# MoE 1's first eight units on whole float32 weights and values, their high and low parts made later

## The chip, the cores and the metric

One Trainium2 chip, one NeuronCore of it (core 0). The metric is the device time of one execution in microseconds (us), the median of the runs. Engines are named as the profile names them: PE multiplies matrices (PEld is its loading of weights, which overlaps), DVE, ACT and POOL work on vectors, SP issues most of the DMA transfers.

## The reference, cut to what matters

```python
# attention: 4 batches, 8 heads, 576 positions, 64 columns a head; heads 0-3 see a window of 32,
# heads 4-7 every fourth position of the last 128
scores = where(mask, q @ k.T / 8, -1e9);  attn = softmax(scores) ;  x = (attn @ v)  -> 2304 x 512
# MoE 1 (w_in 512 x 2048, w_out 2048 x 512, weights arrive as float64)
h = x @ w_in;   g = maximum(h, 0) + alpha * minimum(h, 0);   x = g @ w_out
# MoE 2 (other weights, float64 too)
h = x @ w_in;   g = (a0 + a1 h + a2 h^2 + a3 h^3) / (1 + |b0||h| + |b1|h^2 + 1e-6);   out = g @ w_out
```

## The kernel before

**Three parts, overlapped.** Tokens are cut into 8 chunks of 288 for attention and MoE 1 (`u` = 0 to 7) and 6 chunks of 384 for MoE 2. Attention of one chunk is 4 jobs, one for each pair of heads (`attention_job`). The 2048 columns of `w_in` (rows of `w_out`) are 16 blocks of 128 (`f`). A unit of MoE 1 is one (u, f): 12 matmuls that make `h` (L520), a leaky ReLU on ACT and DVE (L640, L643), and, `LAG1 = 2` units later, 12 matmuls that add into `y` (L673). `SEQ` (L621) is the order of the 128 units: f 0 to 7 for chunk 0 (units n = 0 to 7), f 0 to 7 for chunk 1 (n = 8 to 15), f 8 to 15 for chunk 0 (n = 16 to 23), f 8 to 15 for chunk 1 (n = 24 to 31), then chunks 2 to 7 whole.

**Split products.** Every float32 operand is split into a high part (a copy rounded to float32r, `wh`, `x1h`, `g..h`) and a low part (the rest, `wl`, `x1l`, `g..l`), and a product is three float32r matmuls: low weight by high value, high by low, high by high (L516 to L524 and L669 to L676). So one unit has 4 x 3 matmuls for h and 4 x 3 for y, each 128 x 128 by 288 columns.

**Weights.** They arrive as float64, and a "turn" decodes one: `w64_load` (d) brings the words of w_in for block f and of w_out for block f - 2 into a buffer `raw` (there are `RAWB = 2`, 1 MB each), `w64_exponent` (x, ACT L145) scales the upper words, `w64_sign`, `w64_upper`, `w64_lower` (j, J, i, DVE L151, L158, L164) put the float32 bits into `w`, `w64_hi` (h, ACT L187) and `w64_lo` (l, DVE L197) make `wh` and `wl`. Turns 0 to 17 are MoE 1's, 18 to 35 MoE 2's, whose result goes back to DRAM. h of block f wants turn f, y of block f wants turn f + 2. A `tick` is one step of each kind (L213), and `PACE` (L87) says how many ticks a unit gets: 0.75 up to n = 13, 0.55 up to n = 21, then 0.23. Turns 0 to 3 are decoded in `head()`, in the order of the string `HEAD`.

**Order.** Attention's steps are put into half units by tables (`STEPS`, `EARLY`). Chunk 1's four jobs must end before n = 8. From these program lines a scheduler makes the order on each engine; each engine's queue runs in that order. Rows named `h_0_3` are h of u = 0, f = 3.

Of the kernel before, what the change touches and what calls it, by code (L numbers as in the profile page):

```python
# [22 lines left out]
def tile_attention_moe_moe2(  # L23
# [14 lines left out]
    nc = tc.nc  # L38
# [40 lines left out]
    SPLIT = True  # L79
    NORM_DVE = 3  # L80
    PRE = 3
    W32B = 2
    KEEP = 1
    MAN = ''
    MAN_FROM = 0
    MAN_TO = 128
    PACE = ((14, 0.75), (22, 0.55), (128, 0.23))  # L87

    cst = ctx.enter_context(tc.tile_pool(name="cst", bufs=1))
    wpool = ctx.enter_context(tc.tile_pool(name="wpool", bufs=NF))  # L90
# [68 lines left out]

    def w64_lower(n):
        t, w = raws[n]
        nc.vector.scalar_tensor_tensor(  # L164
            w, t[:, :, 0], 29, w, op0=ALU.logical_shift_right, op1=ALU.bitwise_or
        )
        raws[n] = w.bitcast(F32)
        moe, parts = turns[n]
        if moe == 2:
            for i, (f, part) in enumerate(parts):  # L170
                nc.sync.dma_start(
                    w2f[f, :, part * DM : (part + 1) * DM],
                    w[:, i * DM : (i + 1) * DM].bitcast(F32),
                )

    def w_tiles(moe, f):
        wh[moe, f] = wpool.tile([P, 2 * DM], F32R, tag="wh", name=f"wh{moe}_{f}")
# [2 lines left out]
    def w64_hi(n):  # L180
        moe, parts = turns[n]
        if moe == 1:
            for i, (f, part) in enumerate(parts):
                if (1, f) not in wh:
                    w_tiles(1, f)
                s = slice(part * DM, (part + 1) * DM)
                nc.scalar.activation(  # L187
                    wh[1, f][:, s], raws[n][:, i * DM : (i + 1) * DM], AF.Copy
                )

    def w64_lo(n):
# [86 lines left out]
    def attention_job(mem, u, hp, bk, eng=nc.sync, split=False):  # L278
# [224 lines left out]
        yield  # L503
        if u not in x1:
            x1[u] = x1_tiles(u)
        xh, xl, pxv = x1[u][0][:, hp, :], x1[u][1][:, hp, :], px[:, :C1]
        if dil:
            xh = xh.rearrange("p (i r) -> p r i", r=4)
            xl = xl.rearrange("p (i r) -> p r i", r=4)
            pxv = pxv.rearrange("p (r i) -> p r i", r=4)  # L510
        nc.scalar.activation(xh, pxv, AF.Copy)
        nc.vector.tensor_tensor(xl, pxv, xh.bitcast(F32), op=ALU.subtract)  # L512
        yield


# [10 lines left out]
    if True:  # L526
# [102 lines left out]
        def moe1_h(n):  # L629
            u, f = SEQ[n]  # L630
            ph = bank("h", 2, f"h1_{u}_{f}")
            h_matmuls(ph, C1, wh[1, f], wl[1, f], *x1[u])
            h = ph[:, :C1]
            r = mo1.tile([P, C1], F32, tag="r1", name=f"r1_{u}_{f}")
            ghi, glo = pair(f"g1_{u}_{f}", C1)
            g_tiles[n] = (ghi, glo)
            sg, sa = side[:, f : f + 1], salpha[:, f : f + 1]

# [340 lines left out]
```

## Time and profile before

| what | value |
|---|---|
| device time, median of 3 runs | 977.42 us (972.84 to 978.70) |
| profiled execution, device time | 978.13 us |
| profiled execution, span from first to last instruction | 976.4 us |
| mean granted clock of PE over the span | 0.979 of 2.4 GHz |
| busy share of the span: PE, DVE, ACT, POOL | 96%, 68%, 65%, 22% |

All times in the views count from the start of the span. An instruction's busy time on PE, DVE and ACT includes the end of its pipeline, which overlaps the next instruction of the same engine; the distance between two starts is therefore shorter than the duration printed. A row of a timeline joins like instructions that follow each other ("x4"). PEclk 1.00 is 2.4 GHz, 0.50 is 1.2 GHz.

### The profile page before, as it was taken

The numbers are of one execution on the slowest core, as the hardware profiler recorded it, in microseconds if no ns is written. First come the engines' busy times: TensorE is split into PE (matmuls) and PEld (weight loads), VectorE is DVE, ScalarE is ACT, GpSimd is POOL, SyncE is SP. The second block draws the span as 40 slices with busy tenths as digits, with TensorE's granted clock in tenths as the row PEclk, the third lists the DMA queues.
The fourth block names the chain that finished last, engine by engine and source line by source line (L and its number), as shares of the span: only waits on it lengthen the run. The fifth ranks groups of instructions, "written<-read, shape, count | busy, mean of one in ns | idle before, by whom it ended". The sixth has DMA issues, their size and how long they took to land.

```text
span 976.4 us, 18434 instructions
## 1 busy us (share of the span) xinstructions
PE 937.6 (96%) x6704; PEld 874.4 (90%) x6704; DVE 666.2 (68%) x1578; ACT 632.1 (65%) x1575; POOL 212.7 (22%) x257
## 2 busy tenths in 40 slices
PE   6789899999999999999999999999999999999998
PEld 5678799889899999999999999999999999999996
DVE  2888885556456555554435679877777788777776
ACT  3876665656455565564545578777677776777765
POOL 2000000001000010000112345434343343343332
PEclk7799999999999999999999999999999999999999
DMA  7656535563634535322134432002030020020000
GB/s 182 162 177 178 201 117 161 137 196 97 188 115 119 184 112 162 124 83 83 50 109 136 153 112 66 1 33 65 1 94 4 31 67 1 33 65 1 34 1 33
DMA packets 93899, 94.41 MB, mean 97 GB/s; under 512 B 40176, under 2 KB 81648, under 8 KB 93808
## 3 DMA queue, kind: packets, MB, share of 16 engines
q1 hardware_dynamic: 87360, 83.78, 28.1%
q0 software_dynamic: 6448, 9.45, 3.8%
q8 instruction: 53, 0.87, 0.4%
q14 instruction: 38, 0.31, 0.1%
HBM read 69.48 MB, written 23.72 MB: 95 GB/s over the span
## 4 chain that ended last, share of the span: by engine, by line
PE 83%; ACT 5%; DMA 5%; DVE 4%; issue 1%; SPq 1%; POOL 0%; POOLq 0%; ACTq 0%; DVEq 0%
PE h L520 39%; PE o L892 20%; PE y L673 17%; DMA raw<-in_moe_w_out_dram 3%; PE px L499 2%; PE pp L448 2%; ACT pr L427 1%; PE ps L405 1%; DMA hd<-in_q_dram 1%; PE ps L393 1%; ACT hd L427 1%; DVE w L158 1%; DVE wl L197 1%; DVE w L164 1%; PE pk L356 1%
## 5 line engine op out<-in xcount | busy, mean ns | idle before, releaser
L520 PE MATMUL h<-x1h,wl 128*128 128x288 f32 x512 | 159.3, 312 | 7.0 <-DVE g_0l L649 2.4
L520 PE MATMUL h<-x1l,wh 128*128 128x288 f32 x512 | 154.2, 301 | 0.0
L520 PE MATMUL h<-x1h,wh 128*128 128x288 f32 x512 | 153.5, 300 | 0.0
L643 DVE SCALAR_TENSOR_TENSOR h<-h,salpha,r 128x288 f32<-128x288 f32 x128 | 66.9, 523 | 112.7 <-ACT r L640 112.6
L520 PE MATMUL h<-x2h,wl 128*128 128x384 f32 x384 | 130.4, 340 | 0.0
L520 PE MATMUL h<-x2h,wh 128*128 128x384 f32 x384 | 130.0, 339 | 0.0
L520 PE MATMUL h<-x2l,wh 128*128 128x384 f32 x384 | 129.6, 338 | 0.0
L640 ACT ACTIVATE r<-h,side 128x288 f32<-128x288 f32 x128 | 63.9, 499 | 98.3 <-PE h L520 98.0
L437 POOL TENSOR_TENSOR pr<-pr,sm 128x480 f32<-128x480 f32 (+2 forms) x20 | 23.9, 1197 | 467.5 <-DVE sm L435 416.8
L520 PEld LDWEIGHTS h<-x1h,wl 128*128 128x128 f32 x512 | 98.2, 192 | 11.2 <-DVE g_0l L649 2.6
L824 POOL TENSOR_SCALAR qq<-hh,babs 128x384 f32<-128x384 f32 x96 | 56.7, 591 | 225.3 <-ACT hh L822 225.2
L827 POOL TENSOR_TENSOR qq<-qq,w 128x384 f32<-128x384 f32 x96 | 97.5, 1016 | 8.3 <-POOL qq L824 0.5
L520 PEld LDWEIGHTS h<-x1h,wh 128*128 128x128 f32 x512 | 98.8, 193 | 0.1
L520 PEld LDWEIGHTS h<-x1l,wh 128*128 128x128 f32 x512 | 98.5, 192 | 0.3 <-DVE x1l L512 0.2
L822 ACT ACTIVATE hh<-h 128x384 f32<-128x384 f32 x96 | 47.2, 492 | 62.7 <-PE h L520 62.7
L829 DVE TENSOR_TENSOR t<-h,t 128x384 f32<-128x384 f32 x96 | 53.5, 557 | 48.1 <-ACT t L828 47.6
L520 PEld LDWEIGHTS h<-x2h,wl 128*128 128x128 f32 x384 | 72.0, 188 | 4.0
L520 PEld LDWEIGHTS h<-x2l,wh 128*128 128x128 f32 x384 | 72.1, 188 | 3.6
L838 ACT ACTIVATE w<-qq 128x384 f32<-128x384 f32 (+1 forms) x98 | 50.8, 519 | 33.5 <-POOL qq L827 33.5
L520 PEld LDWEIGHTS h<-x2h,wh 128*128 128x128 f32 x384 | 72.0, 187 | 0.0
L846 DVE TENSOR_TENSOR qq<-qq,w 128x384 f32<-128x384 f32 (+1 forms) x98 | 54.2, 553 | 24.4 <-ACT w L841 24.1
L427 ACT ACTIVATE pr<-pr,mx 128x96 f32<-128x96 f32 (+2 forms) x182 | 65.1, 360 | 5.9 <-DVE mx L419 5.7
(356 smaller groups left out, 2550.2 us busy)
## 6 DMA issues: line engine op xcount, KB each, us to landing
raw<-in_moe_w_in_dram SPq DMA_DIRECT2D x32, 512.0 KB
raw<-in_moe_w_out_dram SPq DMA_DIRECT2D x32, 512.0 KB
w2f<-w SPq DMA_DIRECT2D x32, 256.0 KB
w<-w2f SPq DMA_DIRECT2D x16, 512.0 KB
x2h<-x2hi POOLq DMA_DIRECT2D x6, 768.0 KB, 5.0
x2l<-x2lo POOLq DMA_DIRECT2D x6, 768.0 KB, 6.3
out_dram<-o SPq DMA_DIRECT2D x15, 256.0 KB
tq<-in_q_dram SPq DMA_DIRECT2D x28, 72.0 KB
```

The lines of the kernel that those rows point to most:

```text
L427: nc.scalar.activation(pr[:, j, :], pr[:, j, :], AF.Exp, scale=-1.0, bias=mx[:, j : j + 1], accum_out=sm[:, j : j + 1],)
L520: nc.tensor.matmul(ph[:, :n], lhsT=w_[:, c * P : (c + 1) * P], rhs=x_[:, c, :], start=(i == 0), stop=(i == 3 * KD - 1),)
L640: nc.scalar.activation(r, h, AF.Identity, scale=sg)
L643: nc.vector.scalar_tensor_tensor(h, h, sa, r, op0=ALU.mult, op1=ALU.max)
L673: nc.tensor.matmul(ys[c][:, :C1], lhsT=w_[:, s], rhs=g_, start=begin and i == 0, stop=end and i == 2,)
L822: nc.scalar.activation(hh, h, AF.Square)
L824: nc.gpsimd.tensor_scalar(qq, hh, babs, 1.0 + 1e-6, op0=ALU.mult, op1=ALU.add)
L827: nc.gpsimd.tensor_tensor(qq, qq, w, op=ALU.add)
L829: nc.vector.tensor_tensor(t, h, t, op=ALU.mult)
L838: nc.scalar.activation(w[:, s], qq[:, s], AF.Abs_reciprocal_sqrt, scale=2.0**-44)
L846: nc.vector.tensor_tensor(qq[:, s], qq[:, s], w[:, s], op=ALU.mult)
L892: nc.tensor.matmul(o2[c][i], lhsT=g_, rhs=w_, start=(f == 0 and j == 0), stop=(f == NF - 1 and j == 2),)
```

## The change

Blocks f = 0 to 7 (`FPN = FH = 8`) are first kept as whole float32: `w64_lower` writes its last bits not in place but into a tile `w1_f` (`whole`), in two halves of 512 columns, and `w64_hi` and `w64_lo` leave these blocks out. Chunk 0's attention result is one float32 tile `x1f` without a low part. The units n = 0 to 7 multiply whole float32 operands: one matmul where there were three, for h and for y, and `g` has no low part. From n = 4 on, `w_split` makes `wh` and `wl` of each block, and `x1_split` makes the two parts of chunk 0, which its second half (n = 16 to 23) uses. The buffer `w` is single (`W32B` 2 to 1). `PACE` changes: 0.75 up to n = 7, 0.25 up to n = 15, 0.75 up to n = 23, then 0.22.

```diff
-    W32B = 2
+    W32B = 1
...
-    PACE = ((14, 0.75), (22, 0.55), (128, 0.23))
+    PACE = ((8, 0.75), (16, 0.25), (24, 0.75), (128, 0.22))
+    FPN = FH
...
     def w64_lower(n):
         t, w = raws[n]
-        nc.vector.scalar_tensor_tensor(
-            w, t[:, :, 0], 29, w, op0=ALU.logical_shift_right, op1=ALU.bitwise_or
+        moe, parts = turns[n]
+        lower = lambda to, c: nc.vector.scalar_tensor_tensor(
+            to, t[:, c, 0], 29, w[:, c], op0=ALU.logical_shift_right, op1=ALU.bitwise_or
         )
         raws[n] = w.bitcast(F32)
-        moe, parts = turns[n]
+        if any(moe == 1 and f < FPN for f, _ in parts):
+            for i, (f, part) in enumerate(parts):
+                c = slice(i * DM, (i + 1) * DM)
+                if f < FPN:
+                    if (f, 0) not in whole:
+                        whole_tile(f)
+                    lower(whole[f, part].bitcast(I32), c)
+                else:
+                    lower(w[:, c], c)
+        else:
+            lower(w, slice(None))
...
+    def whole_tile(f):
+        t = wpool.tile([P, 2 * DM], F32, tag="wh", name=f"w1_{f}")
+        whole[f, 0], whole[f, 1] = t[:, :DM], t[:, DM:]
+
+    def w_split(f, part):
+        w = whole.pop((f, part))
+        s = slice(part * DM, (part + 1) * DM)
+        nc.scalar.activation(wh[1, f][:, s], w, AF.Copy)
+        nc.vector.tensor_tensor(
+            wl[1, f][:, s], w, wh[1, f][:, s].bitcast(F32), op=ALU.subtract
+        )
...
             for i, (f, part) in enumerate(parts):
+                if f < FPN:
+                    continue
...
-        nc.vector.tensor_tensor(xl, pxv, xh.bitcast(F32), op=ALU.subtract)
+        if u:
+            nc.vector.tensor_tensor(xl, pxv, xh.bitcast(F32), op=ALU.subtract)
...
-            h_matmuls(ph, C1, wh[1, f], wl[1, f], *x1[u])
             h = ph[:, :C1]
+            if n < FPN:
+                for i, c in enumerate(HPS):
+                    nc.tensor.matmul(
+                        h, lhsT=whole[f, 0][:, c * P : (c + 1) * P],
+                        rhs=x1[u][0][:, c, :],
+                        start=(i == 0), stop=(i == KD - 1),
+                    )
+            else:
+                h_matmuls(ph, C1, wh[1, f], wl[1, f], *x1[u])
...
-            at_half(n + 1, 1, lo)
+            if n >= FPN:
+                at_half(n + 1, 1, lo)
...
             for c in range(KD):
+                if n < FPN:
+                    nc.tensor.matmul(
+                        ys[c][:, :C1], lhsT=whole[f, 1][:, c * P : (c + 1) * P],
+                        rhs=ghi, start=begin, stop=end,
+                    )
+                    continue
...
+        def x1_split(c):
+
+            x, a, b = x1[0][0], *x1s
+            nc.scalar.activation(a[:, c, :], x[:, c, :], AF.Copy)
+            nc.vector.tensor_tensor(
+                b[:, c, :], x[:, c, :], a[:, c, :].bitcast(F32), op=ALU.subtract
+            )
+            if c == KD - 1:
+                x1[0] = (a, b)
...
+        for f in range(FPN):
+            at_half(f + 4, 0, lambda f=f: w_split(f, 0))
+            at_half(f + 5, 1, lambda f=f: w_split(f, 1))
+        for c in range(KD):
+            at_half(FPN + 2 + c, 1, lambda c=c: x1_split(c))
```

How the engines' orders move is shown at three places; line numbers of after are its own.

On PE, where chunk 0's last attention products (px) end and MoE 1's first unit (h_0_0) begins; before:

```order
L499 MATMUL px_2_466<-hd_2_2_106,hd_2_1_105 64x72 x6
L520 MATMUL h_0_0_606<-x1h_430,wl_0_247 128x288
L520 MATMUL h_0_0_606<-x1l_431,wh_0_246 128x288
L520 MATMUL h_0_0_606<-x1h_430,wh_0_246 128x288
L520 MATMUL h_0_0_606<-x1h_430,wl_0_247 128x288
L520 MATMUL h_0_0_606<-x1l_431,wh_0_246 128x288
```

And at the same place after (w_0 is the whole block 0, x1f the whole attention result):

```order
L529 MATMUL px_3_444<-hd_3_2_102,hd_3_1_101 64x72 x6
L668 MATMUL h_0_0_609<-x1f,w_0_195 128x288 x2
L529 MATMUL px_2_453<-hd_2_2_106,hd_2_1_105 64x72 x6
L382 MATMUL pq_0_493<-ident,tq_0_420 128x96 x3
L668 MATMUL h_0_0_609<-x1f,w_0_195 128x288
L386 MATMUL pk_0_494<-ident,tk_0_421 128x80 x4
L668 MATMUL h_0_0_609<-x1f,w_0_195 128x288
L668 MATMUL h_0_1_674<-x1f,w_1_309 128x288
L435 MATMUL ps_0_512<-kT_0_502,qT_0_503 64x96 x10
L668 MATMUL h_0_1_674<-x1f,w_1_309 128x288 x3
L668 MATMUL h_0_2_719<-x1f,w_2_382 128x288 x4
```

Twelve matmuls of h_0_0 became four, and they stand partly ahead of the last px.

On DVE, from the decoding of turn 3 to the first masks of chunk 1's attention (ISA rows); before:

```order
L197 TENSOR_TENSOR wl_2_447<-w_2_361,wh_2_446 128x512
L197 TENSOR_TENSOR wl_0_247<-w_2_361,wh_0_246 128x512
L151 TENSOR_SCALAR w_3_455<-raw_415 128x1024
L512 TENSOR_TENSOR x1l_431<-px_3_457,x1h_430 128x4x72
L512 TENSOR_TENSOR x1l_431<-px_2_466,x1h_430 128x4x72
L158 SCALAR_TENSOR_TENSOR w_3_455<-raw_415,w_3_455 128x1024
L164 SCALAR_TENSOR_TENSOR w_3_455<-raw_415,w_3_455 128x1024
L643 SCALAR_TENSOR_TENSOR h_0_0_606<-h_0_0_606,salpha,r_0_0_619 128x288
L151 TENSOR_SCALAR w_4_654<-raw_481 128x1024
L197 TENSOR_TENSOR wl_3_485<-w_3_455,wh_3_484 128x512
L197 TENSOR_TENSOR wl_1_357<-w_3_455,wh_1_356 128x512
L419 ISA pr_0_506,mx_0_507<-ps_0_509,masks_122 128x96
```

and after:

```order
L154 TENSOR_SCALAR w_3_442<-raw_411 128x1024
L161 SCALAR_TENSOR_TENSOR w_3_442<-raw_411,w_3_442 128x1024
L168 SCALAR_TENSOR_TENSOR w_3_465<-raw_411,w_3_442 128x512
L168 SCALAR_TENSOR_TENSOR w_1_309<-raw_411,w_3_442 128x512
L154 TENSOR_SCALAR w_4_648<-raw_468 128x1024
L449 ISA pr_0_509,mx_0_510<-ps_0_512,masks_122 128x96
```

The subtractions for wl and x1l are gone from here, the last step of the turn is two halves, and the first h is no longer waited for ahead of the masks.

On DVE where h of unit 16 (h_0_8) is worked on; before:

```order
L643 SCALAR_TENSOR_TENSOR h_1_7_1417<-h_1_7_1417,salpha,r_1_7_1430 128x288
L158 SCALAR_TENSOR_TENSOR w_15_1466<-raw_1392,w_15_1466 128x1024
L649 SCALAR_TENSOR_TENSOR g_1_7l<-h_1_7_1417,side,g_1_7h 128x288
L164 SCALAR_TENSOR_TENSOR w_15_1466<-raw_1392,w_15_1466 128x1024
L643 SCALAR_TENSOR_TENSOR h_0_8_1449<-h_0_8_1449,salpha,r_0_8_1462 128x288
L151 TENSOR_SCALAR w_16_1555<-raw_1470 128x512
L197 TENSOR_TENSOR wl_15_1473<-w_15_1466,wh_15_1472 128x512
L197 TENSOR_TENSOR wl_13_1333<-w_15_1466,wh_13_1332 128x512
L649 SCALAR_TENSOR_TENSOR g_0_8l<-h_0_8_1449,side,g_0_8h 128x288
```

and after:

```order
L168 SCALAR_TENSOR_TENSOR w_12_1316<-raw_1259,w_12_1316 128x1024
L694 SCALAR_TENSOR_TENSOR g_1_7l<-h_1_7_1238,side,g_1_7h 128x288
L227 TENSOR_TENSOR wl_12_1324<-w_12_1316,wh_12_1323 128x512
L688 SCALAR_TENSOR_TENSOR h_0_8_1284<-h_0_8_1284,salpha,r_0_8_1297 128x288
L227 TENSOR_TENSOR wl_10_1111<-w_12_1316,wh_10_1110 128x512
L694 SCALAR_TENSOR_TENSOR g_0_8l<-h_0_8_1284,side,g_0_8h 128x288
L154 TENSOR_SCALAR w_13_1391<-raw_1320 128x1024
L161 SCALAR_TENSOR_TENSOR w_13_1391<-raw_1320,w_13_1391 128x1024
L688 SCALAR_TENSOR_TENSOR h_0_9_1330<-h_0_9_1330,salpha,r_0_9_1343 128x288
```

Where turn 15 stood, turn 12 stands now, three turns later; and the first step of a turn (L154) stands behind both subtractions of the turn before, where it stood ahead of them.

## Rows read from the trace of the kernel before

**Rows 1.** Page, parts 1 and 4: busy shares; shares of the last chain.

```profile
PE 937.6 (96%) x6704; PEld 874.4 (90%) x6704; DVE 666.2 (68%) x1578; ACT 632.1 (65%) x1575; POOL 212.7 (22%) x257
...
PE 83%; ACT 5%; DMA 5%; DVE 4%; issue 1%; SPq 1%; POOL 0%; POOLq 0%; ACTq 0%; DVEq 0%
```

**Rows 2.** Windows: start:end, length, busy us (count) per engine, clock, DMA.

```profile
core 0: us, PE busy (x) PEld busy (x) DVE busy (x) ACT busy (x) POOL busy (x), PEclk, DMA share, GB/s
0.00:37.08 37.08, 24.58 (x223) 21.15 (x223) 19.09 (x95) 21.98 (x80) 4.91 (x17) 0.69 0.74 174
37.08:91.62 54.54, 44.71 (x399) 40.10 (x397) 47.01 (x120) 39.92 (x113) 0.00 (x0) 0.90 0.55 167
91.62:124.02 32.40, 27.30 (x195) 25.79 (x195) 29.07 (x49) 19.79 (x41) 0.00 (x0) 1.00 0.62 208
124.02:150.93 26.91, 26.91 (x219) 26.68 (x220) 19.16 (x40) 15.65 (x38) 0.00 (x0) 1.00 0.39 119
150.93:188.52 37.59, 36.13 (x343) 34.15 (x341) 23.28 (x84) 24.36 (x81) 0.00 (x0) 0.95 0.48 134
...
400.00:500.00 100.00, 99.90 (x940) 96.07 (x940) 48.61 (x181) 55.30 (x182) 8.41 (x7) 1.00 0.24 72
```

**Rows 3.** Waits of PE from 37 to 130 us: total, times, longest.

```profile
PE h L520 <- DVE g_0l L649: 2.4, 1, 2.4
PE y L673 <- ACT g_3h L646: 2.3, 1, 2.3
```

**Rows 4.** Last chain from 92 to 125 us: start, us, what.

```profile
103.03 0.38 SPq L131
...
103.47 5.95 DMA raw<-in_moe_w_out_dram
...
109.50 1.15 ACT raw L145
...
115.32 0.38 SPq L131
```

**Rows 5.** Last chain from 31 to 49 us, at chunk 0's last attention steps.

```profile
34.06 1.04 ACT wh L187 x2
...
35.44 1.71 PE px L499 x24
```

**Rows 6.** Timeline of DVE in unit 14: start, duration, instruction, tile, shape.

```profile
115.78 0.69 DVE L151 TENSOR_SCALAR w<-raw 128x1024 int32<-128x1024 int32 x1
116.38 1.29 DVE L197 TENSOR_TENSOR wl<-w,wh 128x512 fp32r<-128x512 f32 x2
117.59 1.22 DVE L158 SCALAR_TENSOR_TENSOR w<-raw,w 128x1024 int32<-128x1024 int32 x1
118.72 0.51 DVE L649 SCALAR_TENSOR_TENSOR g_5l<-h,side,g_5h 128x288 fp32r<-128x288 f32 x1
119.15 1.22 DVE L164 SCALAR_TENSOR_TENSOR w<-raw,w 128x1024 int32<-128x1024 int32 x1
120.28 0.52 DVE L643 SCALAR_TENSOR_TENSOR h<-h,salpha,r 128x288 f32<-128x288 f32 x1
```

**Rows 7.** Timeline of PE: float32r matmuls at half clock, then at full clock.

```profile
38.20 0.44 PE L520 MATMUL h<-x1l,wh 128*128 128x288 f32 x1
38.45 0.44 PE L520 MATMUL h<-x1h,wh 128*128 128x288 f32 x1
...
130.22 0.29 PE L520 MATMUL h<-x1h,wh 128*128 128x288 f32 x1
130.35 0.29 PE L520 MATMUL h<-x1h,wl 128*128 128x288 f32 x1
```

**Rows 8.** Timeline and chain of PE: float32 products (warm, ps) and transposes (pp).

```profile
1.60 5.48 PE L573 MATMUL warm<-ident 128*128 128x128 f32 x24 [1.60 <-POOL ident masks.py:199]
42.85 1.04 PE L405 MATMUL ps<-kT,qT 64*64 64x96 f32 x20
...
142.84 0.55 PE pp L448 x5
```

More of the change, by code (lines that the diff above doesn't have):

```diff
@@ L113, in tile_attention_moe_moe2 @@
     wh, wl = {}, {}
+    whole = {}
     raws = {}
@@ L195, in w64_lo @@
             for i, (f, part) in enumerate(parts):
+                if f < FPN:
+                    continue
                 s = slice(part * DM, (part + 1) * DM)
@@ L505, in attention_job @@
             x1[u] = x1_tiles(u)
-        xh, xl, pxv = x1[u][0][:, hp, :], x1[u][1][:, hp, :], px[:, :C1]
+        xh, xl, pxv = x1[u][0][:, hp, :], x1[u][-1][:, hp, :], px[:, :C1]
         if dil:
@@ L554, in x1_tiles @@
         def x1_tiles(u):
+            if u == 0:
+                return (mo1.tile([P, KD, C1], F32, tag="x1f", name="x1f", bufs=1),)
             return (
@@ L631, in moe1_h @@
             ph = bank("h", 2, f"h1_{u}_{f}")
-            h_matmuls(ph, C1, wh[1, f], wl[1, f], *x1[u])
             h = ph[:, :C1]
-            r = mo1.tile([P, C1], F32, tag="r1", name=f"r1_{u}_{f}")
-            ghi, glo = pair(f"g1_{u}_{f}", C1)
+            if n < FPN:
[7 more added lines that the diff above has]
+                h_matmuls(ph, C1, wh[1, f], wl[1, f], *x1[u])
+            r = mo1.tile([P, C1], F32, tag="r1", name=f"r1_{u}_{f}")
+            if n < FPN:
+                ghi = gy.tile([P, C2], F32R, tag="hi", name=f"g1_{u}_{f}h")
+                ghi, glo = ghi[:, :C1].bitcast(F32), None
+            else:
+                ghi, glo = pair(f"g1_{u}_{f}", C1)
             g_tiles[n] = (ghi, glo)
@@ L668, in moe1_y @@
             for c in range(KD):
+                if n < FPN:
+                    nc.tensor.matmul(
+                        ys[c][:, :C1], lhsT=whole[f, 1][:, c * P : (c + 1) * P],
+                        rhs=ghi, start=begin, stop=end,
+                    )
+                    continue
                 s = slice(DM + c * P, DM + (c + 1) * P)
@@ L709, in moe1_y @@
                 at_half(n + LAG1 + 1, 0, spill if f == NF - 1 else part)
+        def x1_split(c):
[6 more added lines that the diff above has]
+                x1[0] = (a, b)
+        x1s = [
+            mo1.tile([P, KD, C1], F32R, tag=tag, name=tag + "0") for tag in ("x1h", "x1l")
+        ]
+        for f in range(FPN):
+            if (f, 0) not in whole:
+                whole_tile(f)
+        for f in range(FPN):
+            w_tiles(1, f)
+        for f in range(FPN):
+            at_half(f + 4, 0, lambda f=f: w_split(f, 0))
+            at_half(f + 5, 1, lambda f=f: w_split(f, 1))
+        for c in range(KD):
+            at_half(FPN + 2 + c, 1, lambda c=c: x1_split(c))
         att_pe, att_rest = {}, {}
```

## The prediction

> **What bounds the kernel now.** First the page: PE is busy for 96% of the span and holds 83% of the last chain [rows 1]. So an edit pays only where PE stands still or runs at half clock. Next the windows, cut where h of units n = 0, 8, 16, 24 and 32 starts [rows 2]. From 124 us on PE is full (26.91 of 26.91 us; further on 99.90 of 100), while the two windows before it are not: n = 0 to 7 take 54.5 us with DVE busiest (47.0) and the clock at 0.90, n = 8 to 15 take 32.4 us with DVE at 29.1. Unit 14 on DVE shows its price list, each step from its start to the next one's start [rows 6]: a turn of 1024 words costs 0.60 (L151), 1.21 (two wl), 1.13 (L158) and 1.13 (L164), 4.1 us together; L643 and the low part of g cost 0.43 each.
>
> Two different things hold the two windows. In n = 0 to 7 the waits of PE are for low parts on DVE and copies on ACT, none above 2.4 us [rows 3]: four attention jobs, the decoding and the units stand in one queue on each engine. In n = 8 to 15 the last chain is the decode loop: a load is issued at 103.03, its last transfer takes 5.95 us, then exponent, sign, upper, lower, and only then the buffer is free for the next load, at 115.32 [rows 4]: 12.3 us for two turns (two buffers), 6.1 us a turn. At 0.75 turns a unit that is 4.6 us a unit at worst; the window's mean is 32.4 / 8 = 4.05, where PE needs 24 matmuls of 0.132 us = 3.2.
>
> **The whole product.** A float32r matmul of 288 columns starts 0.25 us after the one before at half clock and 0.13 at full clock [rows 7]; I take 0.132, so three cost 0.396. A whole float32 product of this shape isn't in the trace. Bounds [rows 8]: ps, ten float32 products on 64 x 64 tiles, leaves 20 records in 1.04 us, so 0.052 for 96 columns, 2 x 3 x 0.052 = 0.31 us for 288. The 12 warm products leave 24 records in 5.48 us, 0.228 for 128 columns, 2 x 2.25 x 0.228 = 1.03 us. The nearest row in shape and clock is pp, transposes of float32 with one record each: 5 in 0.55 us, 0.11 for 128 columns; two records of 288 columns are 2 x 2.25 x 0.11 = 0.50 us. I take 0.50. The 64 products (8 units x 8) then add 64 x (0.50 - 0.396) = 6.7 us to PE.
>
> The Trainium skill (FP8 and Floating Point Precision, TensorE Precision Notes) speaks against the change: a true float32 product is four passes through the array. By it, with one float32r matmul as a pass, a product is 4 x 0.132 = 0.53 us and PE gains 8.5 us of work instead of 6.7; the two records a product of rows 8 don't contradict it, and the forecast below would be 1.8 us later.
>
> **What leaves, what comes, by stage.** I counted each engine's rows in the two orders and priced them by such rows; the sum is full-clock work without waits.
>
> Head (up to 37.08 us): two wh copies of 1.04 us stand in the chain ahead of the last px [rows 5] and go, as do four wl and four x1l subtractions on DVE. ACT still has its exponentials there. I take 1.2 us earlier, bounds 0.5 and 3.
>
> n = 0 to 7, before: PE 34.9 (8 x 12 matmuls for h and 6 x 12 for y at 0.132, 22.2, and 12.7 of attention), DVE 44.7 (14 wl 8.5; 8 low parts of g 3.4; 7 + 7 + 6 decode steps 18.9; masks, norms, x1l and L643 the rest). It took 54.5, 1.22 times the busiest. After: DVE loses the 8 low parts (3.4), 5 of 14 wl (3.1: the splits of w_split already begin at n = 4), two L151, one L158, gets 1.5 of x1_split and 0.5 for halved L164: 37.1. PE gets 56 x 0.104 = 5.8 and becomes the busiest with 40.7. With a factor near the same, 1.2, the stage takes 49.0: 5.5 less. Between 40.7 x 1.05 (43) and 54 (nothing gained: the attention jobs' chain sets it) all can be. ACT isn't the bound (39.9 of 54.5).
>
> n = 8 to 15: before 32.4 by the loop. After only 3 turns stand here in place of 5 to 6, so the loop is out of the way; DVE is left with 14 wl (the splits of blocks 0 to 7), 3 turns, 16 steps of g: 24.0. PE needs 25.4 + 8 x 0.104 = 26.2. No attention job runs here but the start of one; factor 1.08 (n = 16 to 23 of before has 1.01, n = 0 to 7 1.22): 28.3, 4.1 less. The splits hide under PE with 2 us to spare; if PE were 2 us shorter, they would show.
>
> n = 16 to 23: the decoding put off comes due. DVE 15.9 becomes 25.8 (8 wl for 4, three full turns and two half ones for three half ones). PE 26.6 becomes 27.9, 1.3 of attention having slid in. Factor 1.08: 30.1 against 26.9, 3.2 more. Bounds: 28.2 (PE alone) and 34 (the loop's pace of rows 4 again, for the turns that are full).
>
> n = 24 to 31: PE's work is the same, 33.5; one full turn of MoE 2 leaves DVE. 37.6 becomes 37.1, 0.5 less. From unit 25 on PE's order is row for row the old one, and PE is full [rows 2]; the slower pace of MoE 2's turns (0.22 for 0.23) hides there.
>
> Smaller edits, costed at nothing net: the single `w` makes a turn's first step wait for both subtractions and so for ACT's copies of the turn before; behind it on DVE stand L643 and the low part of g, which PE wants two units later. About 0.2 us a turn, eight turns, covered in n = 8 to 15 by PE; without the cover 1.6 us. The halved L164 adds about 0.1 us eight times, counted above. The loads of turns 10 to 17 now pass SP's queue together with chunk 0's y1p stores and chunk 2's q, k, v; DMA is at 0.39 to 0.62 in these windows [rows 2].
>
> Sum: 1.2 + 5.5 + 4.1 - 3.2 + 0.5 = 8.1 us less. The span of 976.4 becomes 968.3; the profiled execution's device time, 978.13, becomes 970.0. The median of the runs is 0.7 below that execution: 977.4 - 8.1 = 969.3 us.
>
> **Rivals.**
> A, the forecast: 969.3, with 966 to 972 around it. Chance 0.47.
> B, the waits come back: n = 0 to 7 takes 52 (the four attention jobs and the splits put into n = 4 to 7 keep the queues as full: DVE from unit 2 to 8 has as much as before, 33 against 32 us), and n = 16 to 23 takes 32 by the loop. Then 1.2 + 2.5 + 4.1 - 5.1 + 0.5 = 3.2 less: 974. Speaks for it: none of the waits of rows 3 is long, so removing one work shows the next. Against: no unit of the eight waits for a low part of g any more. Chance 0.29.
> C, PE runs dense: without the low parts PE hardly waits, the clock stays at 1.00 after the start: n = 0 to 7 in 43, n = 8 to 15 in 27, n = 16 to 23 in 28.5. 1.2 + 11.5 + 5.4 - 1.6 + 0.5 = 17 less: 960. For it: DVE and ACT drop to 37 and 32 us of work there. Chance 0.14.
> D, the product is as cheap as ps says, 0.31: PE's work in n = 0 to 7 is 34.9 - 56 x 0.086 = 30.1, DVE is the busiest again with 37.1, x 1.22 = 45.3; n = 8 to 15 in 27.5. 1.2 + 9.2 + 4.9 - 3.2 + 0.5 = 12.6 less: 965. Against: the ps records are of quarter tiles, which may lie side by side. Chance 0.06.
> E, slower: the product costs what warm says, 1.03. PE's work in n = 0 to 7 is 34.9 + 56 x 0.634 = 70.4, x 1.05 = 74; n = 8 to 15 gets 5 more. 1.2 - 19.5 - 0.9 - 3.2 + 0.5 = 21.9 more: 999. It decides from 0.50 + 8.1 / 64 = 0.63 us a product on. Against: pp at full clock, and warm is the program's first work. Chance 0.04.
>
> **How the numbers follow.** A measurement of this kernel tells about 1% from no change (its three runs lie 0.6% apart); 1% below 977.4 is 967.6. Faster by over 1%: C and D (0.20) and a third of A (0.16), 0.36. Slower by over 1%: E, 0.04. Within 1%: 0.60. The range reaches down to C and up past B, 960 to 976; E and the lower half of C are left out, about 1 in 8.
>
> **What would show it.** In the windows of after, h of unit 8 starts at 85 (A), 88 (B) or 79 (C); unit 16 at 113, unit 24 at 143, unit 32 at 180. The group of whole products shows two records each, about 0.25 us from start to start at full clock. Waits of PE for a low part in n = 0 to 7 are gone; the last chain of n = 8 to 15 is PE and no longer the transfer of raw. In n = 16 to 23 DVE is busy above 25 us. Wrong would be: records 0.5 us apart (E), or unit 8 no earlier than at 90, which means the attention jobs set that window, or a PE idle by more than 4 us in n = 16 to 23 with a raw transfer at its end, which means that the put-off turns took the gain back.

## The result and the profile after

The changed kernel takes 964.14 us (median of four executions, 960.63 to 966.53) against 977.03 of the kernel before (four, 972.84 to 978.70): a ratio of 0.987, 95% interval 0.983 to 0.992. In a second comparison (six executions, median 961.97, against eleven of before, 975.08) it is 0.986, 0.983 to 0.990. So the change is faster by 1.3 to 1.4%. The forecast of 969.3 was 5.2 us too high for the first comparison. The range of 960 to 976 holds the time; the narrower band around the forecast itself, 966 to 972 (rival A), does not. A change faster by over 1% had a chance of 0.36 and one within 1% had 0.60, so the less likely of the two came.

The profiled execution of after took 964.02 us, 14.1 less than that of before. Each table of stages in this document shows one execution. That of before (978.13 us) is one of its longer ones: 74 executions of this kernel in all comparisons have a median of 975.4 (969.7 to 981.9). So differences of stages against it come out a little larger than differences of the medians. The page's part 1 (busy time and share of each engine) and part 4 (shares of the last chain) answer to [rows 1]:

```profile
PE 936.0 (97%) x6640; PEld 865.9 (90%) x6640; DVE 663.7 (69%) x1578; ACT 631.8 (66%) x1579; POOL 212.9 (22%) x257
...
PE 85%; DMA 5%; ACT 5%; DVE 3%; issue 1%; SPq 0%; POOL 0%; POOLq 0%; ACTq 0%; DVEq 0%
```

PE has 64 records fewer (the 64 whole products leave two records each where the split ones left three) and is busy 1.6 us less. The windows of after, cut where h of units 0, 8, 16, 24, 32, 48 and 64 starts, answer to [rows 2]; the two last ones lie beyond it:

```profile
core 0: us, PE busy (x) PEld busy (x) DVE busy (x) ACT busy (x) POOL busy (x), PEclk, DMA share, GB/s
0.00:35.74 35.74, 22.40 (x210) 19.16 (x210) 16.37 (x90) 19.45 (x75) 4.91 (x17) 0.74 0.75 178
35.74:85.12 49.38, 44.96 (x314) 33.04 (x313) 37.18 (x110) 36.07 (x107) 0.00 (x0) 0.91 0.59 174
85.12:114.65 29.53, 29.53 (x208) 28.08 (x205) 27.60 (x45) 20.21 (x40) 0.00 (x0) 0.94 0.49 160
114.65:143.20 28.55, 28.55 (x243) 28.03 (x242) 26.38 (x52) 21.00 (x48) 0.00 (x0) 1.00 0.43 139
143.20:179.93 36.73, 34.62 (x344) 32.86 (x342) 23.04 (x86) 23.33 (x82) 0.00 (x0) 1.00 0.48 141
179.93:244.80 64.87, 64.30 (x587) 61.42 (x584) 37.46 (x117) 38.76 (x113) 5.13 (x4) 1.00 0.54 160
244.80:308.71 63.91, 63.26 (x585) 60.84 (x584) 34.72 (x111) 37.41 (x112) 4.28 (x4) 1.00 0.43 130
```

The same two last stretches in the kernel before:

```profile
188.52:255.09 66.57, 64.53 (x588) 61.59 (x584) 37.02 (x116) 38.26 (x113) 5.13 (x4) 1.00 0.56 159
255.09:322.22 67.13, 64.86 (x585) 62.22 (x584) 36.29 (x112) 36.62 (x112) 4.28 (x4) 0.97 0.47 142
```

| stage | before | after | moved | forecast |
|---|---|---|---|---|
| head, to h of unit 0 | 37.08 | 35.74 | -1.34 | -1.2 |
| units 0 to 7 | 54.54 | 49.38 | -5.16 | -5.5 |
| units 8 to 15 | 32.40 | 29.53 | -2.87 | -4.1 |
| units 16 to 23 | 26.91 | 28.55 | +1.64 | +3.2 |
| units 24 to 31 | 37.59 | 36.73 | -0.86 | -0.5 |
| sum up to unit 32 | 188.52 | 179.93 | -8.59 | -8.1 |
| units 32 to 63 | 133.70 | 128.78 | -4.92 | 0 |
| unit 64 to the end | 654.2 | 653.5 | -0.7 | 0 |

Up to unit 32 the sum is met within 0.5 us. What was not forecast is the 4.9 us in units 32 to 63, where no line of MoE 1 was changed. There the kernel before has two stalls. These are PE's waits from 188 to 322 us (total, times, longest), one row of PE's timeline, and two of ACT's (in brackets: idle before, and what ended it):

```profile
PE pp L448 <- ACT qT L362: 4.1, 2, 2.3
```

```profile
268.35 0.83 PE L448 MATMUL pp<-ident,pr 128*96 128x128 f32 x4 [2.27 <-ACT qT L362]
```

```profile
266.81 1.10 ACT L145 ACTIVATE raw<-raw 128x1024 f32<-128x1024 f32 x1 [3.01 <-DMA raw<-in_moe_w_out_dram]
267.81 0.39 ACT L362 ACTIVATE qT<-pq 128x288 f32<-128x288 f32 x1
```

ACT's queue stands at the exponent (L145) of a turn of MoE 2 until its transfer has landed; behind it stands qT, a copy for attention, and behind that PE's pp. The other stall, 1.85 us ahead of a pp at 215.49, has the same shape. In after PE waits for none of this from 180 to 309 us:

```profile
PE y L725 <- DVE y_3l L756: 0.7, 1, 0.7
PE pp L478 <- POOL pr L467: 0.6, 2, 0.3
```

The turns moved. By unit 24 the old `PACE` has given 14 x 0.75 + 8 x 0.55 + 2 x 0.23 = 15.36 ticks and the new one 8 x 0.75 + 8 x 0.25 + 8 x 0.75 = 14.0. MoE 2's third to sixth exponents fall into units 29, 29, 37 and 38 in before, in pairs, and into units 34, 37, 39 and 44 in after, one by one.

### The profile page after: what moved, and what is told of

It reads as the page before. It is cut to its first block, busy times and chain, and to the rows that moved or that the text cites. A ratio compares the mean times of both kernels' runs of the same rounds, so it can differ in the third digit from the quotient of the medians.

```text
span 962.2 us, 18305 instructions
## 1 busy us (share of the span) xinstructions
PE 936.0 (97%) x6640; PEld 865.9 (90%) x6640; DVE 663.7 (69%) x1578; ACT 631.8 (66%) x1579; POOL 212.9 (22%) x257
## 3 DMA queue, kind: packets, MB, share of 16 engines
HBM read 69.48 MB, written 23.72 MB: 97 GB/s over the span
## 4 chain that ended last, share of the span: by engine, by line
PE 85%; DMA 5%; ACT 5%; DVE 3%; issue 1%; SPq 0%; POOL 0%; POOLq 0%; ACTq 0%; DVEq 0%
PE h L551 39%; PE o L968 20%; PE y L725 17%; PE px L529 2%; DMA raw<-in_moe_w_out_dram 2%; DMA raw<-in_moe_w_in_dram 2%; PE pp L478 1%; PE ps L435 1%; PE h L668 1%; DMA hd<-in_q_dram 1%; PE ps L423 1%; ACT pr L457 1%; ACT hd L457 1%; PE y L716 1%; DMA x2hi<-y_0h 1%
## 5 line engine op out<-in xcount | busy, mean ns | idle before, releaser
L551 PE MATMUL h<-x1h,wl 128*128 128x288 f32 x480 | 147.2, 307 | 0.6 <-DVE g_9l L694 0.6
L551 PE MATMUL h<-x1l,wh 128*128 128x288 f32 x480 | 142.5, 297 | 0.0
L551 PE MATMUL h<-x1h,wh 128*128 128x288 f32 x480 | 142.0, 296 | 0.0
L551 PEld LDWEIGHTS h<-x1h,wl 128*128 128x128 f32 x480 | 90.5, 189 | 3.2 <-DVE g_9l L694 0.7
L551 PEld LDWEIGHTS h<-x1l,wh 128*128 128x128 f32 x480 | 90.8, 189 | 0.4 <-DVE x1l L543 0.2
L551 PEld LDWEIGHTS h<-x1h,wh 128*128 128x128 f32 x480 | 90.7, 189 | 0.1
```

The lines of the kernel that those rows point to most:

```text
L551: nc.tensor.matmul(ph[:, :n], lhsT=w_[:, c * P : (c + 1) * P], rhs=x_[:, c, :], start=(i == 0), stop=(i == 3 * KD - 1),)
```

## Experiments

Two questions: which part of the change gave which stage, and whether the stalls belong to the place of the turns or to one execution. Stages below are the lengths of units 0 to 7, 8 to 15, 16 to 23 and 24 to 31, and of 32 to 63. All ratios are against the kernel before, run beside each.

**The pace alone.**

The kernel before, with one line changed:

```diff
-    PACE = ((14, 0.75), (22, 0.55), (128, 0.23))
+    PACE = ((8, 0.75), (16, 0.25), (24, 0.75), (128, 0.22))
```

> The kernel before with only the four numbers of PACE changed to those of the change; every unit keeps its three float32r products. Theory P (the pace, not the products, gave the time after unit 32, since it puts the second MoE's decode turns elsewhere): unit 8 starts at 91 to 92 as in the kernel before; units 8 to 15 take about 28 (no transfer of the raw weights in their chain of waits), units 16 to 23 about 29, and from unit 32 to the end 5 to 6 us go as in the changed kernel (782 against 788): together 967 to 971. Rival C (chance: the two stalls of the kernel before at 213 and 266 belong to that one execution): the stretch after unit 32 stays at 788, and the time is 972 to 975. Rival W (one buffer of decoded weights in place of two gave it): 972 to 975 too.

Measured: 965.12 us (962.51 to 967.05), ratio 0.990 (0.986 to 0.993). Its windows:

```profile
36.80:92.43 55.63, 45.91 (x398) 41.37 (x396) 47.14 (x120) 40.10 (x113) 0.00 (x0) 0.88 0.55 166
92.43:118.01 25.58, 25.27 (x190) 25.05 (x189) 23.92 (x36) 16.63 (x32) 0.00 (x0) 1.00 0.62 201
118.01:145.85 27.84, 27.84 (x227) 27.32 (x226) 22.61 (x50) 18.30 (x45) 0.00 (x0) 1.00 0.44 140
145.85:180.38 34.53, 34.53 (x344) 32.99 (x342) 20.61 (x81) 22.36 (x80) 0.00 (x0) 1.00 0.40 117
```

Four numbers of a table give most of the gain. Unit 8 is no earlier, but units 8 to 15 lose 6.8 us, units 24 to 31 lose 3.1 (of which 1.6 did not come back in a second execution of before, shown below), and units 32 to 63 take 128.0, 5.7 less than in before. It ended faster than expected, since I had foreseen neither the 3.1 nor that units 8 to 15 would come down to PE's own work. Unit 32 starts at 180.38, 0.45 us behind the changed kernel's 179.93: all that the whole products won in units 0 to 7 is nearly gone by there.

The same kernel once more, to see whether the rest of the change is worth anything:

> The kernel of e1_before_newpace once more, to see whether the whole products and the single buffer together are worth anything beside the pace: ten executions of the changed kernel have a median of 962.4 (959.7 to 966.5), five of this one 965.1 (962.5 to 967.1). If the 2.7 are real, this is 964 to 967 again, with units 0 to 7 at 54 to 56 and units 8 to 31 at 88; if they are of the executions, 961 to 964.

Measured: 965.22 us (seven executions, 961.86 to 967.45), ratio 0.990 (0.986 to 0.993), units 0 to 7 in 54.30, units 8 to 31 in 88.1. Twelve executions of the pace alone have a median of 965.2, ten of the changed kernel 962.4; drawn again and again from these executions, the difference of the medians lies between 0.9 and 4.4 us in 95 of 100. So whole products and single buffer together are worth about 2.8 us once the pace is changed, and the pace alone about 10. The next experiment shows that the two don't simply add.

**The change without its pace.**

The changed kernel, with one line put back:

```diff
-    PACE = ((8, 0.75), (16, 0.25), (24, 0.75), (128, 0.22))
+    PACE = ((14, 0.75), (22, 0.55), (128, 0.23))
```

> The changed kernel with only PACE put back to the kernel before's three pairs; the first eight units still multiply whole tiles. Theory P: units 0 to 7 take 49 to 50 (the products are unchanged), units 8 to 15 take 31 to 33, with transfers of raw weights in the chain of waits again, units 16 to 23 about 27, and from unit 32 on it takes about 788 as in the kernel before: together 970 to 972. Rival C (chance) or rival W (the single buffer): the stretch after unit 32 stays near 782, and the time is 964 to 967.

Measured: 970.11 us (966.93 to 971.83), ratio 0.995 (0.993 to 0.997). With the old pace the whole products and the single buffer are thus worth 5.3 us (975.4 to 970.1), and the pace is worth 7.7 on top of them (970.1 to 962.4), where it is worth 10.2 without them. The total is what the pace's theory expected, the stages are not. Units 8 to 15 are worse than foreseen, and units 32 to 63 did not go back to 133:

```profile
36.42:84.39 47.97, 44.52 (x314) 32.62 (x312) 37.10 (x110) 36.17 (x107) 0.00 (x0) 0.92 0.58 176
84.39:122.06 37.67, 34.36 (x226) 31.77 (x223) 34.06 (x54) 23.97 (x45) 0.00 (x0) 0.86 0.55 182
...
185.06:249.85 64.79, 64.33 (x586) 61.61 (x584) 37.33 (x116) 38.28 (x114) 5.13 (x4) 1.00 0.55 162
249.85:313.59 63.74, 63.38 (x586) 60.85 (x584) 36.38 (x112) 36.80 (x112) 4.28 (x4) 1.00 0.48 150
```

In units 8 to 15 the old pace's decode steps and the splits of blocks 0 to 7 meet: DVE has 34.1 us of work in 37.7, where after has 27.6 in 29.5, and PE runs at 0.86 of full clock. The new pace gives few turns here and makes up for them in units 16 to 23. The single `w` may have a share too: in the last chain here a load is issued behind the two subtractions of a turn. How the 37.7 divide between splits and buffer was not taken apart. MoE 2's turns stand in the same units as in before (29, 29, 37, 38, 42, 46, 50), and PE waits for qT only 0.2 us in units 32 to 63. For unit 50 the chain says why; the first row is before's transfer there, the second this kernel's (start, us, what):

```profile
259.17 7.55 DMA raw<-in_moe_w_out_dram
```

```profile
253.94 5.49 DMA raw<-in_moe_w_out_dram
```

The exponent stood idle for 0.96 us behind the shorter one and for 3.01 behind the longer, and PE waited 0.2 and 2.3 us. In unit 37 it stood 1.36 us where it stood 3.62 in before, and PE did not wait there. So the place makes the stall possible, and how soon the load lands decides on it. Why the transfer is 2 us shorter in this kernel, with the stores of x2 issued equally far behind it (258.0 and 263.2, both 4.0 us), is open.

**The tail of the pace alone, from either side.** The first kernel keeps before's pace up to unit 13 and has 14.0 ticks by unit 24; the second keeps after's up to unit 15 and has 15.36.

```diff
-    PACE = ((14, 0.75), (22, 0.55), (128, 0.23))
+    PACE = ((14, 0.75), (24, 0.35), (128, 0.22))
```

```diff
-    PACE = ((8, 0.75), (16, 0.25), (24, 0.75), (128, 0.22))
+    PACE = ((8, 0.75), (16, 0.25), (24, 0.92), (128, 0.23))
```

> The kernel before with PACE at ((14, 0.75), (24, 0.35), (128, 0.22)): the first fourteen units run as before, and by unit 24 as many paced ticks are spent as in the changed kernel (14.0 against 15.36), at its last rate. Theory P: units 0 to 13 as before (unit 8 at 91 to 92), units 16 to 23 some 0 to 1 us shorter, and from unit 32 on 782 to 784 with no stall of PE behind a raw transfer at 213 and 266: together 970 to 972. Rival C: 976 to 977, the stretch after unit 32 at 786 to 788 on some executions of either kernel. Rival W: 976 to 977.

> The changed kernel with the last two pairs of PACE at (24, 0.92), (128, 0.23): the first sixteen units run as in the changed kernel, and by unit 24 as many ticks are spent as in the kernel before (15.36), at its last rate. Theory P: units 0 to 15 as in the changed kernel (unit 16 at 114.7), units 16 to 23 about 29, and from unit 32 on 787 to 788, with the waits for raw transfers at the places that the kernel before had them, shifted by 8: together 969 to 970. Rival C or W: the stretch after unit 32 stays at 782, and the time is 964 to 966.

Measured: 965.12 us (964.87 to 967.88), ratio 0.990 (0.987 to 0.994), and 968.07 us (966.35 to 973.12), ratio 0.994 (0.991 to 0.997). Windows of the first from unit 8 on, and its only waits of PE from 181 to 309 us:

```profile
91.81:119.54 27.73, 26.55 (x192) 25.34 (x191) 26.48 (x41) 17.34 (x35) 0.00 (x0) 1.00 0.65 220
119.54:146.84 27.30, 27.30 (x225) 27.07 (x224) 20.04 (x45) 17.50 (x42) 0.00 (x0) 1.00 0.35 108
146.84:181.43 34.59, 34.52 (x344) 32.84 (x342) 20.63 (x81) 22.41 (x80) 0.00 (x0) 1.00 0.41 117
```

```profile
PE pp L448 <- POOL pr L437: 0.6, 2, 0.3
```

From unit 16 on it is the pace-alone kernel within 0.6 us a stage, and units 32 to 63 take 128.0. That is 5 us more gain than expected; again units 8 to 15 (27.7 for 32.4) and 24 to 31 (34.6 for 37.6) were the parts not foreseen. The second kernel has the stall of unit 50 again, in units 32 to 63 of 132.2:

```profile
PE pp L478 <- ACT qT L392: 2.5, 2, 2.3
```

Both signs are those of the pace's theory. The single buffer is out as the cause, since the first kernel has two buffers and no stall. Chance alone is out too, as the totals move with the tail both ways (10.3 us less than before, 5.7 more than after); but in e2_after_oldpace the old places went without the stall, so the place alone does not fix it.

**The kernel before once more.**

> The kernel before, unchanged, once more, to see which of its waits come back in another execution. If the two stalls of the attention's row pp behind a raw transfer (PE idle 1.85 near 213 and 2.3 near 267) belong to the place of the second MoE's turns, units 32 to 63 take 132 to 134 again; if they come and go with the execution, 128 to 130. The loop of decode steps in units 8 to 15 (32.4) returns on either view, and units 24 to 31 take 36 to 38.

Measured: 977.00 us, one execution; units 8 to 15 31.4, units 24 to 31 36.0, units 32 to 63 133.4. Both stalls are back, at the same two turns. The first is 1.0 us long for 1.85, the second 2.9 for 2.27, and the second's transfer took 8.14 us:

```profile
PE pp L448 <- ACT qT L362: 3.8, 2, 2.9
```

```profile
257.57 8.14 DMA raw<-in_moe_w_out_dram
```

Units 24 to 31 differ by 1.6 between the two executions: in the first, PE ran at half clock from 174.2 to 177.6, in this one not.

**The single buffer alone, beside the new pace.**

The kernel of e1_before_newpace, with one line changed:

```diff
-    W32B = 2
+    W32B = 1
```

> The kernel before with the change's PACE, as e1_before_newpace, and one buffer of decoded weights in place of two. Theory B (the single buffer takes back part of what the whole products gain, since a turn's sign step must wait for the last turn's lower step and the raw transfers are issued later): units 8 to 15 take 28 to 30 against 25.6, units 24 to 31 take 36 to 37 against 34.5, and the time is 968 to 970. Theory M (what the whole products gain in units 0 to 7 is paid back by their own matmuls, 64 times (0.485 - 0.396) = 5.7 us of TensorE, once TensorE never waits): the stages stay within 0.5 us of e1_before_newpace, and the time is 964 to 966.

Measured: 971.42 us (967.81 to 972.46), ratio 0.996 (0.994 to 0.998): 6.3 us above the pace alone. Its windows:

```profile
39.12:91.71 52.59, 43.53 (x371) 39.45 (x369) 42.68 (x114) 36.95 (x106) 0.00 (x0) 0.86 0.49 144
91.71:122.77 31.06, 28.55 (x207) 27.80 (x205) 26.11 (x39) 19.11 (x36) 0.00 (x0) 0.95 0.57 182
122.77:152.53 29.76, 28.63 (x239) 27.83 (x238) 26.33 (x53) 18.73 (x45) 0.00 (x0) 1.00 0.46 144
```

The time expected by the buffer's theory was 968 to 970. The head is 2.3 longer than with the pace alone, units 0 to 7 are 3.0 shorter and hold 27 matmuls less, which have slid behind unit 8, and units 8 to 23 take 60.8 against 53.4. PE waits 3.6 us there for steps that come late, where the pace alone has one wait of 0.3:

```profile
PE ps L405 <- ACT kT L363: 2.5, 1, 2.5
PE h L520 <- DVE g_9l L649: 1.1, 1, 1.1
```

Units 24 to 31, which the buffer's theory wanted at 36 to 37, took 34.8. With three products the single buffer is a cost of 6.3; the whole products then win 9.0 (971.4 to 962.4), and the net is the 2.8 above.

**A second buffer beside the whole products.** In these two kernels every other turn from turn 11 on uses the place of x1f, once x1f has been split. The second one's program lines split it in units 8 and 9 in place of 10 to 13. On the engines that changes nothing: the scheduler had put the splits ahead already, at 56.2 to 68.3 us in the first and at 56.6 to 68.5 in the second (in after at 56.9 to 68.8, all before unit 8), and every engine, and SP's queue, runs the same instructions in the same order in both. So the second is a repeat of the first, and its own question, whether a buffer that is free sooner helps, stays unanswered.

Against the changed kernel:

```diff
-                return (mo1.tile([P, KD, C1], F32, tag="x1f", name="x1f", bufs=1),)
+                t = dec.tile([P, KD * C1], I32, tag="w32b", name="x1f")
+                return (t.bitcast(F32).rearrange("p (c t) -> p c t", c=KD),)
...
+        if n >= 11 and n % 2:
+            w = dec.tile([P, KD * C1], I32, tag="w32b", name=f"w32_{n}")
+        else:
+            w = dec.tile([P, 2 * DM], I32, tag="w32", name=f"w32_{n}", bufs=W32B)
```

And in the second one also:

```diff
-            at_half(FPN + 2 + c, 1, lambda c=c: x1_split(c))
+            at_half(FPN + c // 2, c % 2, lambda c=c: x1_split(c))
```

> The changed kernel with a second buffer of decoded weights again from turn 11 on, for every other turn: it is the place where the first chunk's whole values x1f stood, free once unit 13 has split them. Theory B2 (e6_newpace_one has shown 6.3 us for the single buffer, most of it in units 8 to 23, where raw loads and decode steps come late): units 8 to 15 take 27 to 29.5, units 16 to 23 27 to 28, units 24 to 31 34.5 to 35.5, unit 32 starts 2.5 to 4 us before the changed kernel's 179.9, and the time is 960 to 962. Theory M (the whole products' own 5.7 us of TensorE is what takes their gain back, and TensorE has no waits left in units 8 to 23 that a buffer could shorten): units 8 to 23 stay at 58 in all, units 24 to 31 fall at most by the 2.1 that TensorE waits there, and the time is 962 to 964.

> As e8_second, and the first chunk's values are split in units 8 and 9 in place of 10 to 13, so that the second buffer is free four units sooner. Theory B2: the turn 11 near unit 11 finds it free, units 8 to 15 take 26 to 28.5, and the time is 959 to 961. Theory M: as e8_second within 1 us. Against both: the four splits (0.33 on ScalarE and 0.40 on VectorE each) fall on the units in which the weights of units 4 to 7 are split too, and units 8 to 9 get longer by up to 1.5 us, so 961 to 964.

Measured: 960.93 us (960.68 to 962.45) and 961.16 us (960.25 to 965.50), ratios 0.986 (0.983 to 0.990) and 0.987 (0.984 to 0.990). The first was run once more beside the changed kernel:

> The changed kernel, unchanged, once more beside e11_second_again, to tell 964.1 from 960.9. If the second buffer of decoded weights is worth anything, this is 963 to 966, and units 24 to 31 take 36 to 37 with one or two waits of TensorE for the attention's pr or for a low part behind a raw transfer; if the difference was of the executions alone, it is 960 to 962.

> The kernel of e8_second once more. If the second buffer is worth anything, 960 to 962 and 2 to 4 below e10_after_again, with units 24 to 31 at 35 to 36; if not, both agree within 1 us.

Measured: 961.97 (959.73 to 963.43) and 962.00 (961.30 to 962.61). The two agree. All 15 executions with the second buffer have a median of 961.6 and the ten of the changed kernel 962.4; drawn again as above, the difference lies between -0.8 and 2.7 us. So a version that beats the changed kernel is not shown. The stages say what the second buffer moves: units 8 to 23 take 58.1 in the changed kernel, both times, and 58.4 and 58.6 with the second buffer; units 24 to 31 take 36.7 and 37.1 against 35.8 and 35.1. PE's waits there, in the changed kernel (first fence) and in the second run with the buffer:

```profile
PE pp L478 <- DVE pr L467: 1.5, 1, 1.5
PE h L551 <- DVE g_9l L694: 0.6, 1, 0.6
```

```profile
PE pp L481 <- ACT r L689: 0.5, 1, 0.5
```

One to two us are moved there, and no more than that can be read from the total. Beside whole products a second buffer from turn 11 on brings nothing in units 8 to 23, where PE has no wait that it could shorten.

**Half as many whole products.**

Against the changed kernel:

```diff
-    FPN = FH
+    FPN = 4
...
-            at_half(FPN + 2 + c, 1, lambda c=c: x1_split(c))
+            at_half(2 + c // 2, c % 2, lambda c=c: x1_split(c))
```

> The changed kernel with FPN = 4 in place of 8: only units 0 to 3 multiply whole tiles, units 4 to 7 take three products, and x1 of the first chunk is split in units 2 and 3 in place of 10 to 13. Theory M (a whole product costs TensorE 0.485 against 0.396, so 8 units cost 5.7 us and 4 units 2.8, while most of the wait that they save lies in units 0 to 3): unit 8 starts at 86 to 89, and unit 32 at 175.5 to 178, 2.5 to 4 us ahead of the changed kernel: 960 to 962. Theory B (the single buffer): units 8 to 15 and 24 to 31 keep the changed kernel's 29.5 and 36.7, unit 32 starts at 179.5 to 181 and the time is 964 to 966. Rival S (the high and low parts of values and weights that come back into units 0 to 7 stop them again, as in the kernel before): unit 8 at 91 to 92, and 966 to 969.

Measured: 966.76 us (964.04 to 968.07), ratio 0.991 (0.988 to 0.994). The total lies in rival S's range, but none of the three is right in its stages. Unit 8 starts at 94.66, later than in any other kernel, and units 8 to 15 are the shortest of all:

```profile
36.94:94.66 57.72, 51.24 (x381) 40.88 (x379) 46.81 (x122) 42.20 (x118) 0.00 (x0) 0.84 0.55 166
94.66:119.73 25.07, 25.07 (x190) 24.95 (x189) 22.13 (x46) 18.05 (x42) 0.00 (x0) 1.00 0.53 171
119.73:148.50 28.77, 27.84 (x225) 27.11 (x224) 25.95 (x43) 17.16 (x35) 0.00 (x0) 1.00 0.45 144
```

Units 0 to 7 hold 381 matmuls for the changed kernel's 314: 17 more of h and 12 of y for the units of three products (12 matmuls where a whole unit has 8), and 38 of attention, which had slid behind unit 8 there. PE isn't idle much (6.5 us) but runs at 0.84 of full clock, and it waits 2.83 us for the first copy of g after the whole units. At unit 32, 184.72, it is 4.8 us behind the changed kernel. So the gain is not simply the wait in units 0 to 3 less the price of the products; what the whole products of units 4 to 7 add to it was not taken apart further.

## Why the prediction was right, and where it failed

The sum up to unit 32 was right in total (-8.6 for -8.1) and the range held, but in part by luck: the time lies below the forecast's own band, and the range holds it because it was drawn down to the total of rival C, 960. The missing 5 us came from a term that the sum had put at nothing (units 32 to 63, below).

**Head, -1.2.** It came at -1.34; four further executions with whole tiles and x1f in its own place have unit 0 at 36.07 to 36.94, against 37.08 and 37.54 of before and 36.80 to 37.75 of the three runs with before's head and another pace. The means of five are 36.30 and 37.33, so 1.0: right in size; that the two wh copies are the cause was not tested by itself.

**The whole product, 0.50 us.** The timeline of PE has eight records of h back to back:

```profile
65.75 2.10 PE L668 MATMUL h<-x1f,w 128*128 128x288 f32 x8
67.69 1.13 PE L716 MATMUL y<-g_3h,w 128*128 128x288 f32 x4
```

(67.69 - 65.75) / 8 = 0.243 for a record, two records for a product, 0.485 us: the transposes of [rows 8] were the right nearest row, and rivals D and E, which rested on ps and warm, are out. Four times the 0.132 of a float32r matmul, the estimate by the four passes of the Trainium skill (FP8 and Floating Point Precision, TensorE Precision Notes), is 0.53; the measurement is 8% below that. It bears the four passes out all the same: PEclk is 1.00 here, and 0.485 us at 2.4 GHz are 4.04 clocks for each of the 288 columns, where the 0.132 of a float32r matmul are 1.10. So the 8% lie in taking a float32r matmul for one pass. The 64 products add 64 x (0.485 - 0.396) = 5.7 us to PE where 6.7 was taken. One sum ahead of it is off without effect: the items for DVE in units 0 to 7 after come to 37.9, not 37.1 (44.7 - 3.4 - 3.1 - 1.2 - 1.1 + 1.5 + 0.5); PE was taken as the busiest there, with 40.7.

**Units 0 to 7, -5.5.** -5.16 in this profile, 48.29 us in the second. No unit waits for a low part, as said. What is left of PE's waits from 35.7 to 85.2 us, in place of [rows 3]:

```profile
PE px L529 <- ACT pT L484: 2.3, 1, 2.3
PE pq L382 <- ACT pT L484: 1.1, 1, 1.1
PE h L668 <- ACT g_0h L691: 1.0, 1, 1.0
```

The size is right, and its meaning was not. The prediction took it as a gain to keep. Against the pace alone, the changed kernel is 7.3 us ahead at unit 8 and 0.45 at unit 32. Of the 6.9 lost between, some 3.0 (what the other two parts leave) are real work put off: units 8 to 23 hold 451 matmuls in the changed kernel and 417 with the pace alone, with no more of MoE 1 among them (378 and 383). The forecast counted 1.3 us of attention sliding into units 16 to 23 only. In after PE is full in units 8 to 23, so what slides there is paid in full. The rest is 1.7 us of half clock in units 8 to 15 (85.7 to 89.1) and 2.2 in units 24 to 31, where the pace alone has no wait of PE and the changed kernel has the two shown above.

**Units 8 to 15, -4.1, and 16 to 23, +3.2.** The loop of [rows 4] is gone and the last chain there (85 to 115 us in after) is PE's own rows, as said:

```profile
by line: PE h L551 49.9%; PE y L725 31.6%; PE y L716 13.1%; PE px L529 3.5%; PE ps L435 1.0%; PE pq L382 0.8%; PE pk L386 0.8%
```

Both terms were too large: -2.87 and +1.64, in sum -1.2 against -0.9. In units 8 to 15 the half clock after the wait of 2.29 us at 84.84 costs 1.7, more than the 1.2 that are missing. In units 16 to 23 PE was full (28.55 of 28.55) where a factor of 1.08 on its work was taken, so the put-off decoding, DVE at 26.4 us, hides altogether. The pace did this, not the products: it makes units 8 to 15 6.8 shorter and 16 to 23 0.9 longer without them.

**Units 24 to 31, -0.5.** -0.86, as a difference of larger things: the moved turns give 3.1 (pace alone; 1.5 against the second execution of before), the whole products and the single buffer take 2.2 back.

**Later, 0: the step that failed.** "From unit 25 on PE's order is row for row the old one, and PE is full [rows 2]; the slower pace of MoE 2's turns (0.22 for 0.23) hides there." The order is the old one, but PE was not full in units 32 to 63, nor from 150.93 to 188.52 us, where [rows 2] itself has 36.13 of 37.59. The row that stood for it was the window from 400 to 500 us, which holds only the last two of MoE 2's exponents in before (at 408.0 and 423.8), while ten stand between 170 and 325 us; and [rows 3], the waits, end at 130 us. The same view from 200 to 300 us in before reads:

```profile
200.00:300.00 100.00, 95.69 (x877) 91.08 (x876) 54.71 (x174) 55.53 (x170) 7.27 (x6) 0.98 0.49 145
```

The two windows and the waits of pp shown in the first section hold 4.1 us of PE idle behind raw transfers and 1.7 of half clock after one of them (269.8 to 273.2): 5.8, against 133.7 - 128.0 = 5.7 that the tail of the pace alone took away. And the rate, 0.22 for 0.23, is the smaller part of the move: by unit 50 it makes 26 x 0.01 = 0.26 tick, while 1.36 are missing by unit 24 already. Together they set each later turn some units back and break up the pairs; no run changed one without the other.

**The rivals.** B (the waits come back) had unit 8 at 88 and the loop in units 16 to 23; neither came. C had unit 8 at 79 and a full clock: its total, 960, is nearer to both measurements than the forecast is, but not by its mechanism. D's 965 is nearest of all to the first, at a price of the product that the rows rule out. The forecast A had the signs: unit 8 at 85.1 (85), unit 16 at 114.7 (113), unit 24 at 143.2 (143), unit 32 at 179.9 (180).

## What to carry to other kernels

When a change moves a table that paces background work, follow each moved step to the place where it now stands, through the whole program, and read the waits there, not only in the stages that the change names; a window without such steps says nothing of them. Run the table alone and the rewrite alone: here the table alone gave about 10 of 13 us and the rewrite alone 5, so they don't add. Of the 7 us that the rewrite was ahead at unit 8 beside the new table, nearly all was gone 24 units later, in part as work that had slid to where the bounding engine had no gaps left. And a stall behind a shared in-order queue has two conditions, the place of the waiting step and the time of its transfer, so one profile of each kernel doesn't tell what the place alone does.

## What the runs showed of the hardware

- A load of a turn (two transfers of 512 kB) took 5.49 to 8.14 us from the second one's issue to its landing in unit 50, in kernels with the same neighbours in the queue, and 9.72 in unit 37 of before, where the loads of two turns and of attention's inputs follow each other. ACT reached the exponent of unit 50 some 4.6 us behind that issue (263.80 against 259.17 in before, 258.55 against 253.94 in e2_after_oldpace), and PE waited 2.26 to 2.9 us behind the transfers of 7.53 to 8.14 (before, e4_after_tail, e5_before_again) and 0.2 behind the one of 5.49 (e2_after_oldpace).
- Where PE stood for 2.3 to 2.9 us in an otherwise full stretch, 3.4 us at 1.2 GHz followed: after the waits that ended at 268.35 in before, 84.84 in after, 260.62 in e4_after_tail, 267.34 in e5_before_again and 69.48 in e7_four_one. The granted clock in after's stretch:

```profile
85.70:89.10 3.40, 3.40 (x24) 3.25 (x21) 2.40 (x4) 0.70 (x1) 0.00 (x0) 0.50 0.44 119
```

  After the wait of 1.85 us that ended at 215.49 in before, and after one of 2.0 in units 24 to 31 of e10_after_again, the clock stayed at 1.00. But the length of one wait does not decide alone: in before two waits of 0.96 and 0.50 us, with 0.44 of work between them, stood ahead of the 3.4 us at half clock from 174.2. So a wait of some 2.3 us cost 4.0: itself, and half of 3.4.
